# A product with V cut in two, ended by the products of 1/sum, and a new order table

## The chip, the cores and the metric

The kernel runs on one core of one Trainium2 chip. The metric is the device time of one execution in microseconds (us). Before the change it was 1055.64 us, the median of three runs (1054.31 to 1058.27).

The core has five engines that run side by side and meet only at semaphores. In profiles they are PE (TensorE, matrix products; its weight loads are shown as PEld), DVE (VectorE), ACT (ScalarE), POOL (GpSimd) and SP (SyncE, which issues transfers). Each runs its own instructions in a fixed order.

## The reference

An attention with rotary embedding over 8 batches of 8 heads (576 positions, 64 per head), and behind it a channel mix with squared ReLU and a sigmoid gate:

```python
scores = scale * np.matmul(q_rot, k_rot.transpose(0, 1, 3, 2))
scores = scores - np.max(scores, axis=-1, keepdims=True)
attn = np.exp(scores)
attn = attn / (np.sum(attn, axis=-1, keepdims=True) + 1e-09)
x = np.matmul(attn, v)          # then the heads side by side: (8, 576, 512)
...
xk = mu_k * x + (1.0 - mu_k) * x_prev      # x_prev: one position earlier
xr = mu_r * x + (1.0 - mu_r) * x_prev
k = np.maximum(xk @ w_k, 0.0)
v = k * k @ w_v
r = 1.0 / (1.0 + np.exp(-(xr @ w_r)))
return r * v
```

All arrays are float32.

## The kernel before

Attention works on 32 pairs of heads, four pairs to a batch; the channel mix works on 16 half batches of 288 positions. Below, V1 to V32 are the products with V of the 32 pairs.

For each pair, `plan_rope` loads k and q and rotates them (L328 to L332; the operations go through the helper `combine`, L241). `plan_unit` is one of five units of scores: matmuls on TensorE into PSUM tiles `s` (L373), their row maximum on VectorE (L382, tile `nm`), the exponential and its sum on ScalarE (L385, tile `p`), and a transpose of 32x32 blocks on VectorE (L388). `plan_ratio` makes 1/sum and spreads it into the tile `rw` (L413 to L417). `plan_values` multiplies with V: 144 calls of `matmul` on 32-row tiles (L447), which the trace shows as 288 matmuls and 288 weight loads, and then eight calls that spread 1/sum over PSUM in the same way (L454). `plan_total` copies the spread 1/sum to SBUF (ScalarE, L467, tile `rp`), multiplies it with the product (VectorE, L472 to L474, tile `xT`), and hands on the border column (POOL, L479 to L483).

In the channel mix, `plan_mix` forms mu*x + (1-mu)*x_prev and splits it into a high and a low part (L517 to L522, L245, L247, L241), and `plan_product` multiplies with the weights, three matmuls for each step of the sum: high by high, low by high, high by low (L547 to L549, tile `acc`). The weights come as 64-bit words; `plan_convert` turns each of 20 blocks into a high and a low float32 part with eight instructions on VectorE, ScalarE and POOL (L278 to L295 and the helpers).

The order on each engine comes out of a planner. Each operation has a rank: a due time of its pair or half batch (18 rank units a pair), and an offset for its kind from the table `R`. `Plan.issue` plays the program through with a planned duration for each operation and, whenever an engine is free, gives it the ready operation of the lowest rank. Where an operation may run on several engines, it goes to the one that takes it first, with the `B_` numbers as a handicap. Operations marked as shared use the SBUF read interface that VectorE and POOL have in common: in the plan one of them starts only when the other's has ended. Buffers are granted in the order of rank: three PSUM tiles `s`, of which a product with V takes two, and a single tile for V (`vs`).

The lines that set the order and the two parts of the product:

```python
_, i = heapq.heappop(queue)
...
o = op("T", t, 2 * NB * 137 + 330, values, need, slots + [d["sp"], d["sv"]])
o = op("T", t + 0.01, 2 * 137, shares, [o, d["R"]], slots + [d["srw"]])
```

Of the kernel before, what the change touches and what calls it, by code (L numbers as in the profile page):

```python
# [13 lines left out]
F32 = mybir.dt.float32  # L14
# [10 lines left out]
R = dict(k=28.88, q=62.36, v=55.38, cs=-59.77, ld=36.87, rope0=-101.48, rope1=58.83, rope2=-126.74, split0=-113.91,  # L25
         split1=433.88, u0=-9.3, u1=-10.62, u2=4.58, u3=-7.12, u4=4.34, mx=2.38, ex=86.96, rs=95.84, dg=-55.12,
         bd=122, tr=-72.26, ev=352.37, av=9.08, tot=24.45, bor=5.22, m0=68.43, mh=-2.22, mk=13.02, mr=26.57, ms=1.29,
         tp=149.1, rz=62.63, rc=93.12, mx1=-27.44, mx2=-52.23, mx3=35.89, mg=3.02, mv=-2.35, dr=-78.45, key0=8.16,
         key1=19.5, key2=110.59, gate0=-83.54, gate1=264.13, wk0=-8.35, wk1=-9.74, wr0=-255.69, wr1=-10.63, wv0=-20.6,
         wv1=9.46)  # L30
PB = (-68.11, -8.23, -7.76, -4.01, -5.06, -7.72, 1.05, -20.98)
B_COPY, B_ROPE, B_SPLIT, B_LOW, B_MIX, B_SQUARE, B_RELU, B_SMALL = -365.18, 42.18, -112.3, 217.28, 11.6, -103.75, 494.08, 91.52
MB = (14.69, 13.58, 6.65, 1.17, 2.36, 19.06, 26.3, 392.46)
CY = 12
BUFS = dict(nat=2, kh=2, kl=2, qh=2, ql=2, vs=1, pt=2, s=3, nm=6, sums=2, rs=2, rw=1, rp=2, xT0=4, xT1=4, last=5, raw=1, we=1, wm=1, mxf=2, mxh=5, mxl=5, acc=2, hr=2, kkh=8, kkl=8, rt=3)
# [18 lines left out]
def pool(n):  # L54
    return 2.15 * n + 160

# [7 lines left out]
class Plan:  # L64
# [15 lines left out]
    def op(self, engine, rank, cost, fn, after=(), uses=()):  # L80
# [10 lines left out]
        self.ops.append((engine, rank, None, fn, tuple(after), tuple(uses), opens))  # L91
# [7 lines left out]
    def issue(self):  # L99
# [23 lines left out]
        now, engine = 0.0, {}  # L123

# [67 lines left out]
def rope_attention_channel_mix(ctx, tc, qt, kt, v, cs, mu, w_k, w_v, w_r, out):  # L192
# [28 lines left out]
    def f32(ap):  # L221
        return ap.bitcast(F32)
# [77 lines left out]
    def plan_weights(w, hi, lo, t0, t1):  # L300
# [5 lines left out]
            (c, n): plan_convert(t0 + i * (t1 - t0) / len(blocks), words[c * P:(c + 1) * P, 2 * n:2 * n + 1024], hi[:, c, n:n + 512], lo[:, c, n:n + 512])  # L306
# [6 lines left out]
    def plan_rope(t, d, n, src, plain):  # L313
# [395 lines left out]
```

## Time and profile before

| | |
|---|---|
| median of three runs | 1055.64 us |
| the profiled execution, whole | 1059.64 us |
| its span, first to last instruction | 1057.8 us |
| mean granted clock of TensorE | 0.955 |
| instructions | 34,697 |
| TensorE idle in the span | 100.7 us (1057.8 - 957.1) |
| of that up to 165 us | 67.2 us (165.0 - 97.77) |
| read from HBM, written | 88.74 MB, 9.44 MB |

The page gives, for each engine, its busy time and its number of instructions, and the span in 40 slices of 26.4 us, where a digit is the busy share in tenths. A group row reads: line, engine, operation, what it writes and what it reads, shapes, count; then busy us and the mean of one in ns; then the idle time of the engine just before and what ended it. "issue" stands where the engine waited for nothing that the profile shows.

### The profile page before, as it was taken

What the parts mean: (1) busy time and instruction counts of PE and PEld (TensorE: products, weight loads), DVE (VectorE), ACT (ScalarE), POOL (GpSimd) and SP (SyncE); (2) the same over time, 40 slices, a digit from 0 to 9 for tenths busy, and PEclk for the clock granted to TensorE, in tenths of its full rate; (3) what the DMA queues carried; (4) which work ended last, traced back from release to release, by engine and by line L of the source; (5) the groups of instructions that cost most, each with busy time, mean ns of one, the idle gap of its engine ahead of it and who ended that gap; (6) DMA issues with size and microseconds to landing.
All of it is one profiled execution on the core that took longest, in us unless ns stands there. A gap on an engine that the chain in (4) does not pass through costs nothing.

```text
span 1057.8 us, 34697 instructions
## 1 busy us (share of the span) xinstructions
PE 957.1 (90%) x15134; PEld 841.9 (80%) x15134; DVE 845.9 (80%) x1483; ACT 537.0 (51%) x1330; POOL 479.9 (45%) x556
## 2 busy tenths in 40 slices
PE   2676478999899999999999999999999999999998
PEld 1454256878788888888888888888888888988998
DVE  7898889869498888788788887778887988776552
ACT  2343436637175565537475555546474655645243
POOL 5544336445264463536374464437453535322111
PEclk9957667999999999999999999999999999999999
DMA  6333332241312233132322233132322233211000
GB/s 246 112 127 130 133 128 85 72 158 41 140 55 105 106 99 111 53 133 73 108 94 79 94 106 105 53 133 78 134 72 72 94 106 105 82 59 54 18 23 24
DMA packets 30456, 100.41 MB, mean 95 GB/s; under 512 B 3040, under 2 KB 11232, under 8 KB 26208
## 3 DMA queue, kind: packets, MB, share of 16 engines
q1 hardware_dynamic: 30304, 98.19, 26.6%
q8 instruction: 119, 1.95, 0.8%
q14 instruction: 33, 0.27, 0.1%
HBM read 88.74 MB, written 9.44 MB: 93 GB/s over the span
## 4 chain that ended last, share of the span: by engine, by line
PE 79%; DVE 13%; issue 4%; ACT 2%; DMA 1%; POOL 1%; DVEq 0%; POOLq 0%; ACTq 0%
PE av L447 18%; PE acc L547 17%; PE acc L548 14%; PE acc L549 14%; PE s L373 13%; DVE nm L382 3%; DVE p L388 2%; PE av L454 2%; ACT p L385 1%; DVE wm L294 1%; DMA raw<-in_w_r 1%; DVE wm L295 1%; DVE mxf L522 1%; DVE wm L282 1%; DVE we L278 1%
## 5 line engine op out<-in xcount | busy, mean ns | idle before, releaser
L385 ACT ACTIVATE p<-s,nm 128x576 f32<-128x576 f32 x288 | 211.4, 737 | 133.6 <-DVE nm L382 132.0
L447 PE MATMUL av<-p,values 32*64 32x160 f32 (+1 forms) x9216 | 192.3, 305 | 38.3 <-issue 22.6
L447 PEld LDWEIGHTS av<-p,values 32*64 32x64 f32 x9216 | 171.9, 136 | 56.5 <-issue 36.2
L382 DVE TENSOR_REDUCE nm<-s 128x1 f32<-128x576 f32 x288 | 205.3, 744 | 14.0 <-PE s L373 13.0
L388 DVE STREAM_TRANSPOSE p<-p 128x576 f32<-128x576 f32 x288 | 210.1, 752 | 5.0 <-ACT p L385 4.8
L373 PE MATMUL s<-kh,qh 64*128 64x288 f32 (+1 forms) x738 | 147.5, 438 | 49.2 <-POOL qh L241 29.0
L547 PE MATMUL acc<-mxh,wk_h 128*128 128x288 f32 x512 | 160.5, 313 | 3.0 <-DVE rt L603 1.4
L547 PE MATMUL acc<-kkh,wv_h 128*128 128x288 f32 x512 | 159.2, 311 | 1.5 <-DVE rt L603 0.9
L373 PEld LDWEIGHTS s<-kh,qh 64*128 64x128 f32 (+1 forms) x738 | 81.9, 212 | 97.6 <-ACT p L385 32.0
L549 PE MATMUL acc<-mxh,wk_l 128*128 128x288 f32 x512 | 151.5, 296 | 1.3 <-POOL wk_l L241 1.3
L548 PE MATMUL acc<-mxl,wk_h 128*128 128x288 f32 x512 | 152.1, 297 | 0.2 <-POOL mxl L241 0.2
L548 PE MATMUL acc<-kkl,wv_h 128*128 128x288 f32 x512 | 151.5, 296 | 0.0
L549 PE MATMUL acc<-kkh,wv_l 128*128 128x288 f32 x512 | 151.2, 295 | 0.0
L241 POOL TENSOR_TENSOR mxl<-mxf,mxh 128x288 fp32r<-128x288 f32 x89 | 79.1, 900 | 100.7 <-DVE mxh L247 71.2
L547 PEld LDWEIGHTS acc<-mxh,wk_h 128*128 128x128 f32 x512 | 96.9, 189 | 20.4 <-issue 14.0
L547 PEld LDWEIGHTS acc<-kkh,wv_h 128*128 128x128 f32 x512 | 96.4, 188 | 16.8 <-issue 11.1
L241 POOL TENSOR_TENSOR kkl<-hr,kkh 128x288 fp32r<-128x288 f32 x95 | 85.7, 910 | 35.6 <-ACT kkh L245 22.2
L467 ACT COPY rp<-av 128x320 f32<-128x320 f32 x64 | 25.1, 428 | 144.6 <-PE av L454 144.1
L549 PEld LDWEIGHTS acc<-mxh,wk_l 128*128 128x128 f32 x512 | 97.0, 189 | 1.7 <-POOL wk_l L241 1.7
L548 PEld LDWEIGHTS acc<-mxl,wk_h 128*128 128x128 f32 x512 | 97.2, 190 | 0.6 <-POOL mxl L241 0.4
L548 PEld LDWEIGHTS acc<-kkl,wv_h 128*128 128x128 f32 x512 | 96.8, 189 | 0.1
L549 PEld LDWEIGHTS acc<-kkh,wv_l 128*128 128x128 f32 x512 | 96.7, 189 | 0.0
(91 smaller groups left out, 1772.1 us busy)
## 6 DMA issues: line engine op xcount, KB each, us to landing
values<-in_v SPq DMA_DIRECT2D x32, 1152.0 KB, 5.1
xq<-in_qt SPq DMA_DIRECT2D x32, 640.0 KB, 4.5
xk<-in_kt SPq DMA_DIRECT2D x32, 576.0 KB, 4.2
out_dram<-rt SPq DMA_DIRECT2D x64, 144.0 KB, 1.8
raw<-in_w_v SPq DMA_DIRECT2D x8, 512.0 KB, 3.2
raw<-in_w_k SPq DMA_DIRECT2D x8, 512.0 KB, 3.3
raw<-in_w_r SPq DMA_DIRECT2D x4, 512.0 KB, 3.3
turn<-in_cs SPq DMA_DIRECT2D x1, 640.0 KB, 4.4
```

The source lines that it names most:

```text
L241: (V if e == "V" else G).tensor_tensor(out=out, in0=a, in1=b, op=op)
L278: V.tensor_scalar(out=u("e"), in0=d["high"], scalar1=20, scalar2=0x7FF, op0=ALU.logical_shift_right, op1=ALU.bitwise_and)
L373: T.matmul(w[x][:, h, 0:H], lhsT=kind(d[q][r, c * P:(c + 1) * P]), rhs=kind(d[k][r, h * H:(h + 1) * H]), start=i == 0, stop=i == len(todo) ...
L382: V.tensor_reduce(out=w["nm", x], in_=w[x][:, :, 0:H], op=ALU.max, axis=AX.XY, negate=True)
L385: A.activation(halves(d["pt"][:, place]), w[x][:, :, 0:H], AF.Exp, bias=w["nm", x], scale=1.0, accum_out=d["sums"][:, place + 1:place + 2])
L388: V.transpose(d["pt"][:, place], d["pt"][:, place])
L447: T.matmul(at(a, x, c0, 32 * (p1 - p0)), lhsT=d["vf"][g, b * P + x * D:b * P + x * D + D], rhs=d["pt"][g, p0:p1, 32 * b:32 * b + 32], star ...
L454: T.matmul(at(a, x, 256, 160), lhsT=first_row[g], rhs=d["rw"][g, p0 + 1:p1 + 1], start=True, stop=True)
L467: A.copy(w["r", half], w[half][:, :, 256:416])
L547: T.matmul(w["a"], lhsT=w_h[:, i, sl], rhs=x["h"], start=(i == 0), stop=False)
L548: T.matmul(w["a"], lhsT=w_h[:, i, sl], rhs=x["l"], start=False, stop=False)
L549: T.matmul(w["a"], lhsT=w_l[:, i, sl], rhs=x["h"], start=False, stop=(i == count - 1))
```

## The change

Four things are changed.

1. The 144 calls of the product with V are two operations of the planner: blocks 0 to 8 (72 calls) and blocks 9 to 17 with the eight products of 1/sum behind them. The second has a rank of its own (`av2`) and waits for 1/sum. Before, the first operation held all 144 calls, and only the eight products waited for 1/sum.
2. When `Plan.issue` picks for VectorE or POOL, each shared operation is ranked later by 0.1353 units for each ns that the other engine will still hold the interface.
3. The first six pairs have offsets of their own for 19 kinds of operation (`EARLY`), and each of the 20 weight blocks has one (`WORDS`); the numbers of `R`, `PB`, `MB` and the handicaps are new.
4. The planned duration of a product on TensorE follows a model of the array (half rate while cold, a cost for a new tile shape, a least time for each 256 instructions), and some planned durations on ScalarE and VectorE differ. That alters only the order.

What is computed is the same, instruction for instruction on TensorE; on VectorE, ScalarE and POOL operations move between engines.

```diff
-R = dict(k=28.88, q=62.36, v=55.38, cs=-59.77, ld=36.87, rope0=-101.48, rope1=58.83, rope2=-126.74, split0=-113.91,
+R = dict(k=44.27, q=66.09, v=57.3, cs=-364.48, ld=64.17, rope0=112.51, rope1=437.99, rope2=-790.69, split0=-68.32,
...
+NE = 6
+EARLY = dict(k=(-430.77, -247.46, -0.16, -62.14, -67.11, -4.22), q=(-124.45, -334.75, -23.13, -18.46, 21.08, 35.02),
...
+WORDS = dict(wk=(-119.65, 277.59, -356.19, -160.94, -146.41, 45.43, 67.45, -152.52), wr=(-120.79, -322.22, -307.35,
...
+CUT = 9
+WAIT = 0.1353
...
+def lead(name, pair):
+    return R[name] + (EARLY[name][pair] if pair < NE else 0)
...
-                    _, i = heapq.heappop(queue)
+                    if e in port:
+                        held = max(0.0, port["G" if e == "V" else "V"] - now)
+                        best = min(queue, key=lambda r: (r[0] + (WAIT * held if r[1] not in engine and ops[r[1]][0][e][2] else 0), r[1]))
+                        queue.remove(best)
+                        heapq.heapify(queue)
+                        _, i = best
+                    else:
+                        _, i = heapq.heappop(queue)
...
+                    if e == "T":
+                        cost = product_time(start, cost, ops[i][2])
...
-        def values():
-            for half in range(2):
-                w[half] = ps.tile([P, 2, 512], F32, tag="s", name="av", bufs=BUFS["s"])
-            for b in range(NB):
+        def values(b0, b1):
+            if b0 == 0:
+                for half in range(2):
+                    w[half] = ps.tile([P, 2, 512], F32, tag="s", name="av", bufs=BUFS["s"])
+            for b in range(b0, b1):
...
-        o = op("T", t, 2 * NB * 137 + 330, values, need, slots + [d["sp"], d["sv"]])
-        o = op("T", t + 0.01, 2 * 137, shares, [o, d["R"]], slots + [d["srw"]])
+        def rest():
+            values(CUT, NB)
+            shares()
+
+        o = op("T", t, 2 * CUT * 144, lambda: values(0, CUT), need, slots + [d["sp"], d["sv"]], ("row", 32 * CUT))
+        o = op("T", t + lead("av2", d["pi"]), 2 * (NB - CUT) * 144 + 2 * 137, rest, [o, d["R"]], slots + [d["sp"], d["sv"], d["srw"]], ("row", 32 * (NB - CUT) + 32))
```

`product_time` is the new model: it takes the planned cost of one TensorE operation and returns the planned time.

```python
def product_time(start, cost, shape):
    kind, count = shape
    ...
    if not array["warm"]:
        cost *= 1.9
    end = start + 220 * (kind != array["shape"])
    array["shape"] = kind
    while count:
        step = min(count, 256 - array["place"])
        end += cost * step / shape[1]
        count -= step
        array["place"] += step
        if array["place"] == 256:
            array["place"] = 0
            end = max(end, array["line"])
            array["line"] = end + 3000
    ...
    return end - start
```

Three places show how the orders differ. The changed file has other line numbers: L432 there is L373, L441 is L382, L447 is L388, L479 is L420, L476 is L417, L507 is L447, L514 is L454, L536 to L538 are L472 to L474, L611 to L613 are L547 to L549, L299 and L305 are the helpers L241 and L247, and L336, L340, L344, L352 and L353 are L278, L282, L286, L294 and L295.

First, TensorE at the end of V16, in the middle of the span. Before, three weight matmuls stand between the 144 calls with V and the eight calls with `first_row`, which spread 1/sum:

```order
L447 MATMUL av<-p,values 64x128
L447 MATMUL av<-p,values 64x160
L547 MATMUL acc<-kkh,wv_h 128x288
L548 MATMUL acc<-kkl,wv_h 128x288
L549 MATMUL acc<-kkh,wv_l 128x288
L454 MATMUL av<-rw,first_row 64x160 x8
L547 MATMUL acc<-mxh,wk_h 128x288
```

In the changed program the three stand in the middle of V16, between its two halves; the eight calls with `first_row` follow the second half directly:

```order
L507 MATMUL av<-p,values 64x128
L507 MATMUL av<-p,values 64x160
L611 MATMUL acc<-kkh,wv_h 128x288
L612 MATMUL acc<-kkl,wv_h 128x288
L613 MATMUL acc<-kkh,wv_l 128x288
L507 MATMUL av<-p,values 64x160
L507 MATMUL av<-p,values 64x128
```

The group of three has moved from behind the product into it; it is so from V5 to V32, while the halves of V1 to V4 touch.

Second, TensorE between V3 and V4. Before, 26 score matmuls follow V3, 18 of pair 4 and then eight of pair 5, and V4 comes behind them:

```order
L454 MATMUL av<-rw,first_row 64x160 x8
L373 MATMUL s<-kh,qh 128x288 x26
L447 MATMUL av<-p,values 64x160
L447 MATMUL av<-p,values 64x128
L447 MATMUL av<-p,values 64x160
```

In the changed program the score matmuls of pair 4 end directly ahead of V4, and six weight matmuls stand among them:

```order
L514 MATMUL av<-rw,first_row 64x160 x8
L432 MATMUL s<-kh,qh 128x288 x8
L611 MATMUL acc<-mxh,wk_h 128x288
L612 MATMUL acc<-mxl,wk_h 128x288
L613 MATMUL acc<-mxh,wk_l 128x288
L432 MATMUL s<-kh,qh 128x288 x6
L611 MATMUL acc<-mxh,wk_h 128x288
L612 MATMUL acc<-mxl,wk_h 128x288
L613 MATMUL acc<-mxh,wk_l 128x288
L432 MATMUL s<-kh,qh 128x288 x4
```

The score matmuls of pair 5 have moved behind V4, and the first weight matmuls ahead of it (before, the first of all stand behind V4).

Third, VectorE ahead of the totals of pair 4 (the first `xT` row of each piece, which needs V4). Before, the last transposes of pair 4 stand 29 instructions earlier, and the maxima and transposes shown here are those of pair 5:

```order
L388 STREAM_TRANSPOSE p<-p 128x576
L241 TENSOR_TENSOR xk<-xk,turn 128x576
L382 TENSOR_REDUCE nm<-s 128x1 x2
L388 STREAM_TRANSPOSE p<-p 128x576 x3
L278 TENSOR_SCALAR we<-raw 128x512
L282 TENSOR_SCALAR wm<-raw 128x512
L294 SCALAR_TENSOR_TENSOR wm<-raw,wm 128x512
L295 SCALAR_TENSOR_TENSOR wm<-raw,wm 128x512
L286 TENSOR_TENSOR wm<-wm,we 128x512
L247 CAST wk_h<-wm 128x512
L241 TENSOR_TENSOR wk_l<-wm,wk_h 128x512
L472 TENSOR_TENSOR xT_1361<-av,rp 128x2x128
```

In the changed program the transpose in the first row is the last of pair 4, and nine instructions stand between it and the totals:

```order
L447 STREAM_TRANSPOSE p<-p 128x576
L305 CAST wk_h<-wm 128x512
L299 TENSOR_TENSOR wk_l<-wm,wk_h 128x512
L299 TENSOR_TENSOR xk<-xk,turn 128x576 x2
L336 TENSOR_SCALAR we<-raw 128x512
L340 TENSOR_SCALAR wm<-raw 128x512
L352 SCALAR_TENSOR_TENSOR wm<-raw,wm 128x512
L353 SCALAR_TENSOR_TENSOR wm<-raw,wm 128x512
L344 TENSOR_TENSOR wm<-wm,we 128x512
L536 TENSOR_TENSOR xT_1358<-av,rp 128x2x128
```

The maxima and transposes of pair 5 have moved behind the totals of pair 4; the conversion of weights fills the place.

More of the change, by code (lines that the diff above doesn't have):

```diff
@@ L78, in slot, with op @@
         return slots[-1]
-    def op(self, engine, rank, cost, fn, after=(), uses=()):
+    def op(self, engine, rank, cost, fn, after=(), uses=(), shape=("full", 0)):
         o = len(self.ops)
@@ L90, in op @@
             s.opener = o
-        self.ops.append((engine, rank, None, fn, tuple(after), tuple(uses), opens))
+        self.ops.append((engine, rank, shape, fn, tuple(after), tuple(uses), opens))
         return o
@@ L123, in issue @@
         now, engine = 0.0, {}
+        array = dict(shape="full", place=0, line=0.0, warm=False, window=0, busy={})
+        def product_time(start, cost, shape):
+            kind, count = shape
+            window = int(start // 3413)
+            for w in range(array["window"], window):
+                share = array["busy"].get(w, 0.0) / 3413
+                array["warm"] = share > 0.95 or share > 0.6 and array["warm"]
+            array["window"] = window
+            if not array["warm"]:
[11 more added lines that the diff above has]
+                    array["line"] = end + 3000
+            at = start
+            while at < end:
+                w = int(at // 3413)
+                to = min(end, (w + 1) * 3413)
+                array["busy"][w] = array["busy"].get(w, 0.0) + to - at
+                at = to
+            return end - start
         def met(i):
@@ L335, in plan_rope @@
         sl = Slot(n + "l")
[L336 removed]
+        r = op(two(w, B_ROPE), t + lead("rope2", pi), 0, lambda e: combine(e, m["c"], m["c"], m["s"], ALU.add), [ms, mc], [slot])
         h = op(one(w, B_SPLIT), t + R["split0"], 0, lambda e: copy(e, part(n + "h"), m["c"]), [r], [slot, sh])
@@ L373, in products @@
                         T.matmul(w[x][:, h, 0:H], lhsT=kind(d[q][r, c * P:(c + 1) * P]), rhs=kind(d[k][r, h * H:(h + 1) * H]), start=i == 0, stop=i == len(todo) - 1)
-        m = op("T", t, (8 if d["plain"] else 6) * (120 + 14) + (360 if c < 4 else 0), products, d["q"] + d["k"], slots + d["sq"] + d["sk"])
+        m = op("T", t, (8 if d["plain"] else 6) * (120 + 12), products, d["q"] + d["k"], slots + d["sq"] + d["sk"], ("row" if c < 4 else "full", (8 if d["plain"] else 12) * len(heads)))
         for x in heads:
@@ L483, in border @@
                 G.tensor_copy(xT[:, 0:1], d["last"])
-        o = op("A", t + R["rc"] + 0.1 * half, act(320) + 60, copied, [o], [slot, s_r])
-        o = op("V", t + R["tot"] + 0.1 * half, dve(256) + 2 * 105, total, [o], [slot, s_r, sx])
+        o = op("A", t + lead("rc", d["pi"]) + 0.1 * half, act(320) + 60, copied, [o], [slot, s_r])
+        o = op("V", t + lead("tot", d["pi"]) + 0.1 * half, dve(256) + 2 * 210 + 30, total, [o], [slot, s_r, sx])
         if half == 0:
@@ L553, in plan_product @@
             x, h, l, s_h, s_l = hold[parts, i]
-            prev = [op("T", t + i * dt, pe(n, 3), lambda i=i, x=x: group(i, x), [h, l, done[i, m * P // 512 * 512]] + prev, [s_a, s_h, s_l])]
+            prev = [op("T", t + i * dt, pe(n, 3), lambda i=i, x=x: group(i, x), [h, l, done[i, m * P // 512 * 512]] + prev, [s_a, s_h, s_l], ("full", 6))]
         return w, s_a, prev[0], t + count * dt
@@ L633, in rope_attention_channel_mix @@
     plan_attention()
-    wk_done = plan_weights(w_k, wk_h, wk_l, R["wk0"], R["wk1"])
-    wr_done = plan_weights(w_r, wr_h, wr_l, R["wr0"], R["wr1"])
-    wv_done = plan_weights(w_v, wv_h, wv_l, R["wv0"], R["wv1"])
+    wk_done = plan_weights(w_k, wk_h, wk_l, R["wk0"], R["wk1"], "wk")
+    wr_done = plan_weights(w_r, wr_h, wr_l, R["wr0"], R["wr1"], "wr")
+    wv_done = plan_weights(w_v, wv_h, wv_l, R["wv0"], R["wv1"], "wv")
     for b in range(B):
```

67 lines of the change are left out of this document (39 added, 28 removed).

## The prediction

> **What bounds the kernel now.** I first read the page's busy shares and slices, to see which engine is full and when.
>
> ```profile
> PE 957.1 (90%) x15134; PEld 841.9 (80%) x15134; DVE 845.9 (80%) x1483; ACT 537.0 (51%) x1330; POOL 479.9 (45%) x556
> PE   2676478999899999999999999999999999999998
> PEclk9957667999999999999999999999999999999999
> q8 instruction: 119, 1.95, 0.8%
> ```
>
> TensorE is full from the eighth slice on; in the first seven (185 us) it idles, partly at a low granted clock. The average of 90% therefore joins two stages. The table by stretches, cut where the products change, separates them (its columns are stretch, length, then busy us and count for PE, PEld, DVE, ACT and POOL, and the clock).
>
> ```profile
> 0.00:165.00 165.00, 97.77 (x1397) 65.23 (x1397) 142.13 (x216) 63.23 (x136) 78.26 (x82) 0.75 0.40 143
> 165.00:215.00 50.00, 45.88 (x573) 40.04 (x579) 45.99 (x78) 31.67 (x75) 26.82 (x28) 0.95 0.24 80
> 215.00:261.00 46.00, 43.64 (x550) 36.59 (x540) 36.73 (x59) 24.95 (x66) 21.06 (x25) 0.96 0.28 99
> 261.00:347.00 86.00, 82.19 (x1372) 72.46 (x1370) 66.10 (x123) 41.52 (x105) 41.97 (x48) 0.98 0.29 100
> 347.00:977.00 630.00, 610.27 (x10617) 551.17 (x10616) 516.55 (x925) 347.93 (x884) 299.01 (x360) 1.00 0.27 92
> ```
>
> Up to 165 us TensorE loses 67 us and VectorE is 86% busy: the start belongs to VectorE. From 347 us TensorE is 97% busy, so only its own work and its own stalls count there. Third view: what TensorE waited for, over the whole span (total, times, longest).
>
> ```profile
> PE s L373 <- POOL qh L241: 29.0, 3, 15.9
> PE av L447 <- issue: 22.6, 30, 2.2
> PE s L373 <- ACT p L385: 16.4, 12, 2.8
> PE av L447 <- DVE p L388: 12.1, 2, 6.7
> PE av L454 <- issue: 3.6, 6, 1.3
> PE acc L547 <- DVE rt L603: 2.3, 7, 0.7
> ```
>
> The waits for other engines are almost all of the start. The 26.2 us called "issue" are different: inside the product with V, TensorE stops although all its data is there, some 30 times. The timeline of one product (start, duration, instructions merged) shows how.
>
> ```profile
> 278.63 2.94 PE L447 MATMUL av<-p,values 32*64 32x160 f32 x153
> 282.07 2.42 PE L447 MATMUL av<-p,values 32*64 32x128 f32 x128 [0.50 <-issue]
> 285.52 0.50 PE L447 MATMUL av<-p,values 32*64 32x128 f32 x7 [1.03 <-issue]
> 285.95 0.40 PE L547 MATMUL acc<-kkh,wv_h 128*128 128x288 f32 x1
> ```
>
> The two stops are exactly 128 matmuls apart. Each matmul has a weight load, so that is 256 instructions, and 30,268 matmuls and loads over the 119 instruction transfers of queue q8 are 254 per transfer. I read this as TensorE outrunning its instruction supply: 128 of these matmuls take 2.42 us, while the next block came 3.45 us after the one before (285.52 - 282.07).
>
> [...]
>
> **The change, part by part.**
>
> *Split of the product with V.* A block filled with these matmuls alone lacks 3.45 - 2.42 = 1.0 us, less what TensorE's queue had in hand (0.50 us lost at the first stop, 1.03 at the second). Counting 256-instruction blocks along both orders, with the phase of the stops above, after the first five products: before has 35 blocks of V matmuls alone and 11 with one group of three weight matmuls; the change has 20 and 28. So the 22.6 us on L447 are some 0.6 us for each block of the first kind, and L454's 3.6 us some 0.3 for each of the second. If those prices held, the saving would be 15 x 0.6 - 17 x 0.3 = 4 us. But before's second kind mostly came after a stop, with nothing in hand; in the change it comes first in the burst, and the group of weight matmuls (0.6 us: 0.5 from 542.62 to a step past 542.99 in the rows below, 0.1 for the change into it) fills most of the gap. At no loss there and 0.6 for the rest the saving is 26 - 12 = 14 us. I take 9, the middle; the ends are 4 and 14.
>
> *The wait for 1/sum ahead of the second half.* Queued behind it on TensorE are the half itself and all that follows. No row shows L447 or L454 waiting for rw, and 1/sum stands at most seven VectorE instructions behind the last transpose in both orders. Its cover is the first half and the weight group, some 3 us. I price it at nothing; if VectorE were that late, each 1 us would cost up to 1 us in each of 32 products.
>
> *More changes between products.* TensorE changes tile shape 388 times instead of 359; 14 of the 29 lie behind the tenth product with V, where nothing hides them.
>
> ```profile
> 541.27 0.29 PE L548 MATMUL acc<-mxl,wk_h 128*128 128x288 f32 x1
> 541.40 0.29 PE L549 MATMUL acc<-mxh,wk_l 128*128 128x288 f32 x1
> 541.63 0.53 PE L373 MATMUL s<-kh,qh 64*128 64x288 f32 x4
> 542.62 0.40 PE L547 MATMUL acc<-mxh,wk_h 128*128 128x288 f32 x1
> 542.86 0.30 PE L548 MATMUL acc<-mxl,wk_h 128*128 128x288 f32 x1
> 542.99 0.29 PE L549 MATMUL acc<-mxh,wk_l 128*128 128x288 f32 x1
> ```
>
> Weight matmuls step 0.13 us; at a change the step is 0.23 and 0.24, so 0.1 more. 14 to 29 changes cost 1.4 to 2.9 us: **+2**.
>
> *The start.* The sixth product with V (V6) is where TensorE last stands directly behind VectorE:
>
> ```profile
> 213.78 0.78 DVE L388 STREAM_TRANSPOSE p<-p 128x576 f32<-128x576 f32 x1 [0.27 <-ACT p L385]
> 214.80 3.33 PE L447 MATMUL av<-p,values 32*64 32x160 f32 x177
> ```
>
> Ahead of that transpose VectorE has 291 instructions before and 284 in the change. Priced by their groups' means they come to 201.6 and 200.1 us (overlap counted twice): **-1.5**. What those instructions lose to POOL is larger:
>
> ```profile
> L282 DVE TENSOR_SCALAR wm<-raw x20: 403/416/1767, 4.4 to 196.0; 128x512 uint32<-128x512 uint32 x20
> L388 DVE STREAM_TRANSPOSE p<-p x288: 710/762/781, 22.3 to 971.7; 128x576 f32<-128x576 f32 x144
> L294 DVE SCALAR_TENSOR_TENSOR wm<-raw,wm x20: 641/682/1916, 4.8 to 196.8; 128x512 uint32<-128x512 uint32 x20
> ...
> L294 DVE SCALAR_TENSOR_TENSOR wm<-raw,wm 128x512 uint32<-128x512 uint32 x20 | 17.0, 848 | 0.2
> L282 DVE TENSOR_SCALAR wm<-raw 128x512 uint32<-128x512 uint32 x20 | 14.1, 707 | 0.0
> L278 DVE TENSOR_SCALAR we<-raw 128x512 uint32<-128x512 uint32 x20 | 13.6, 679 | 3.7 <-DMA raw<-in_w_r 3.6
> ```
>
> The first three rows give the shortest, median and longest of a line, the others count, busy us and mean. L388 is never stretched; L282 runs from 403 to 1767 ns. Against a median of 416 its 20 lose 5.8 us, L278's likewise 5.3, and L294's 3.3: 14.4 us on 60 instructions, 0.24 each. Some 140 of the 291 are of the kinds that the planner marks as sharing the interface (136 in the change), so about 33 us are lost by V6. [...]
>
> The new rule of the planner passes over such instructions while the other engine holds the interface. It acts on planned times, and it can only pick others that are ready. I take a third of the loss, **-11**; the ends are -25 (three quarters of it) and +8 (planned gaps that do not fall where planned). The wait of VectorE for POOL or ScalarE at the totals I leave as it is: in pair 1 the order puts ten instructions ahead of L472 instead of five, but in pair 4 only nine instead of 29.
>
> Against this, the change has done fewer weight matmuls by V6, 192 instead of 219, and as many (735) by V10. These 27 come later at 0.133 us each: **+3.6**. Before, ten score matmuls stand ahead of V4 and wait for POOL, with V4's own operands done:
>
> ```profile
> 125.87 2.08 DVE L388 STREAM_TRANSPOSE p<-p 128x576 f32<-128x576 f32 x3
> 135.32 3.24 PE L373 MATMUL s<-kh,qh 64*128 64x288 f32 x10 [12.31 <-POOL qh L241]
> 141.54 0.79 PE L447 MATMUL av<-p,values 32*64 32x160 f32 x4
> ```
>
> In the change those of pair 5 stand behind V4. That brings weight work forward into the idle start, but V6 waits for VectorE all the same, so I give it nothing. The first product, V1, now waits for more transposes (30 score matmuls ahead of it, not 18); this too lies ahead of V6.
>
> *Moved work and transfers.* VectorE gives 43 instructions away, mostly to ScalarE and POOL (25 more on POOL). Behind 347 us TensorE's 610 of 630 us cover it, worth nothing; were that cover gone, POOL's 25 at the 0.91 us of its most frequent form would cost 23. SP issues the same loads in another order, the early ones above all, and the values tile is held a weight group longer ahead of its next load of 5.1 us; the products with V are 33 us apart (1057.8 / 32), so I price this at nothing too.
>
> ```profile
> L241 POOL TENSOR_TENSOR kkl<-hr,kkh 128x288 fp32r<-128x288 f32 x95 | 85.7, 910 | 35.6 <-ACT kkh L245 22.2
> values<-in_v SPq DMA_DIRECT2D x32, 1152.0 KB, 5.1
> ```
>
>
> **The sum.** -9 + 2 - 1.5 - 11 + 3.6 = -16. The profiled execution took 1059.64 us (span 1057.8), 4.0 above the median of 1055.64: it becomes 1043.6, and on the median's scale **1040**.
>
> **The rivals.**
>
> *The start stays.* Planned gaps miss, VectorE loses 33 us as before: -9 + 2 - 1.5 + 3.6 = -5, so 1051. For it: the trace does not run as planned. In the first 215 us VectorE sat idle for 12.5 us ahead of totals that its order put too early:
>
> ```profile
> DVE xT L472 <- ACT rp L467: 12.5, 4, 4.6
> ```
>
> 16%.
>
> *Most of the interface wait goes.* -25 in place of -11: 1026. For it: half of VectorE's work in the start does not share, so there is often something to pick. 15%.
>
> *The stops only move.* If what a burst no longer waits for is waited for in its second half or behind it, the split is worth 0: -7, so 1049. The 128 matmuls between the rows at 282.07 and 285.52 speak against it. [...] 5%.
>
> *Slower: V6 comes later.* Between V5 and V6 the change leaves TensorE 51 weight matmuls, not 105, some 7 us of work at full clock. So each us by which VectorE is late there is an idle us of TensorE, with a low clock behind it. If the interface loss grows instead of shrinking, it decides from +5 on, where the saved stops are used up; at half as much again (+17) the sum is +12, 1068. For it: POOL is given more to do. Against it: 136 sharing instructions, not more. 8%.
>
> **How the numbers follow.** My forecast holds 56%, with 1032 to 1048 as its own range. What a measurement of this kernel can tell from no change is about 0.5%, 5.3 us: faster is below 1050.4. The forecast, the second and third rival and half of the first make 84%; the other half of the first is 8% within; the last 8%. The range, 1022 to 1054, reaches through the first rival and nearly to the second's centre and leaves out about 6% below and 10% above.
>
> **What would show it.** The split: "PE av L447 <- issue" falls from 22.6 to some 13 us. The start: V6 begins near 202 us, and L282's mean falls from 707 toward 600 ns. Later: no row of the second half waiting for rw, and TensorE at 97% from V10 on. I am wrong if stops stay near 22 us, if V6 lies behind 215, or if TensorE shows waits for other engines after V10.

## The result, and the profile after

| | before | after |
|---|---|---|
| median of four runs each | 1056.95 us | **1027.61 us** (1026.29 to 1029.71) |
| ratio, with its 95% interval | | 0.9721 [0.9683, 0.9759] |
| the profiled execution, whole | 1059.64 us | 1027.46 us |
| its span | 1057.8 us | 1025.6 us |
| mean granted clock | 0.955 | 0.970 |
| V6 begins, V10 begins | 214.8, 347.0 us | 199.1, 327.6 us |

The change gains 2.8%, about 29 us by the medians and 32.2 us between the two profiled executions. Of those 32.2 us, 15.7 are there when V6 begins, 3.7 more when V10 begins (347.0 - 327.6 = 19.4 together), and 12.9 come behind V10 (from V10 to the end 710.8 us before, 697.9 after). Times and ratios, here and below, leave out one execution of `more_vector_late` that took 4874 us; all others lie within 1.5% of the fastest of their kernel.

The page of the changed kernel: busy time of each engine, TensorE's slices and granted clock, and the instruction queue.

```profile
PE 940.8 (92%) x15134; PEld 836.7 (82%) x15134; DVE 834.6 (81%) x1440; ACT 544.6 (53%) x1348; POOL 498.1 (49%) x581
PE   2667687999999999999999999999999999999998
PEclk9987668999999999999999999999999999999999
q8 instruction: 119, 1.95, 0.8%
```

TensorE's program has the same 15,134 matmuls, and 16.3 us less busy time (957.1 - 940.8). The low digits end about as early as before, but fewer of them stand below 9. The table by stretches, cut where V6 and V10 begin, first of the kernel before, then of the changed one (stretch, length, busy us and count of PE, PEld, DVE, ACT and POOL, granted clock, DMA share, GB/s).

```profile
0.00:214.80 214.80, 143.45 (x1956) 105.07 (x1956) 187.92 (x293) 94.89 (x211) 105.08 (x109) 0.79 0.36 128
214.80:347.00 132.20, 126.03 (x1921) 109.26 (x1920) 103.03 (x181) 66.47 (x170) 63.03 (x72) 0.97 0.29 100
```

```profile
0.00:199.12 199.12, 135.41 (x1928) 101.22 (x1928) 180.44 (x291) 86.18 (x199) 97.85 (x108) 0.85 0.41 142
199.12:327.60 128.48, 125.38 (x1946) 110.26 (x1945) 107.10 (x183) 71.25 (x181) 66.71 (x77) 1.00 0.28 98
...
347.00:945.00 598.00, 584.21 (x10212) 532.41 (x10213) 495.97 (x862) 350.35 (x880) 309.90 (x366) 1.00 0.27 94
```

Up to V6, VectorE has nearly the same number of instructions (293 and 291), is busy for 7.5 us less with them and idle for 8.2 us less (26.9 and 18.7 us). TensorE is idle 7.6 us less and runs at a higher clock. From V6 to V10 its clock is 1.00 instead of 0.97, which is worth less than 2 us (`start_old` below takes 130.4 us there, in the order of before and at a clock of 1.00). Behind V10 TensorE is 97.7% busy.

What TensorE waited for, in the changed kernel, from the start to 347 us and from there on (total, times, longest); first the early part.

```profile
PE av L507 <- DVE p L447: 18.3, 5, 5.0
PE s L432 <- POOL qh L299: 17.2, 1, 17.2
PE s L432 <- ACT p L444: 10.4, 9, 1.9
PE acc L611 <- DVE wk_h L305: 6.3, 1, 6.3
```

```profile
PE av L514 <- issue: 10.3, 9, 1.6
PE av L507 <- issue: 2.2, 8, 0.6
PE acc L612 <- issue: 1.0, 1, 1.0
PE acc L611 <- DVE rt L667: 0.2, 1, 0.2
```

Two of the three waits for the rotated q (qh) are gone: 29.0 us in three waits became 17.2 in one. Late in the span the other engines make TensorE wait for 0.4 us in all; what is left are the stops called "issue", and they now stand mostly in the products of 1/sum (L514), no longer in the product with V (L507). Over the whole span they were 3.6 us in the products of 1/sum and 22.6 in the product with V; now they are

```profile
PE av L514 <- issue: 13.5, 13, 1.6
PE av L507 <- issue: 4.6, 10, 1.4
```

No row names rw, and in the trace rw is done 3.1 us or more before any second half begins, so the wait for 1/sum costs nothing. The timeline of V17 shows the new place of a stop (start, duration, instructions merged).

```profile
521.74 2.73 PE L507 MATMUL av<-p,values 32*64 32x160 f32 x144
524.39 0.40 PE L611 MATMUL acc<-mxh,wr_h 128*128 128x288 f32 x1
...
524.99 2.82 PE L507 MATMUL av<-p,values 32*64 32x160 f32 x142
...
527.74 0.34 PE L514 MATMUL av<-rw,first_row 32*64 32x160 f32 x5
529.37 0.49 PE L514 MATMUL av<-rw,first_row 32*64 32x160 f32 x4 [1.29 <-issue]
529.78 0.40 PE L611 MATMUL acc<-mxh,wr_h 128*128 128x288 f32 x1
```

Each half runs through without a stop. Then TensorE stops: the last four products of 1/sum begin 1.63 us after the five before them, and 1.40 us after an instruction transfer that lands at 527.97. The profile calls 1.29 us of that idle. Not every product has this stop: V6 takes 6.4 us in all, V17 8.0 (529.78 - 521.74), and the products behind V10 take either 6.3 to 6.9 us or 7.7 to 8.4.

That these stops are waits for instructions can be seen in the trace, which has the start and the duration of each of the 119 instruction transfers of queue q8. Every one of the 23 idle stops called "issue" on L507 and L514, and every one of the 36 of the kernel before, ends 1.2 to 1.6 us after such a transfer has landed; a random instant of the kernel before lies 0 to 33 us behind the last landing, 4.5 in the median. The 3.45 us between two blocks in the prediction's timeline also come apart: from 282.07 it is 1.1 us until the next transfer starts, the transfer takes 0.9, and 1.4 us after its landing TensorE goes on at 285.52.

The last place where TensorE stands behind VectorE has also moved. Two rows of VectorE's timeline, and two of TensorE's:

```profile
162.34 1.64 DVE L305 CAST wk_h<-wm 128x512 fp32r<-128x512 f32 x1
...
189.52 0.43 DVE L305 CAST wv_h<-wm 128x512 fp32r<-128x512 f32 x1
...
194.89 0.78 DVE L447 STREAM_TRANSPOSE p<-p 128x576 f32<-128x576 f32 x1 [0.40 <-ACT p L444]
```

```profile
164.13 0.58 PE L611 MATMUL acc<-mxh,wk_h 128*128 128x288 f32 x1 [6.31 <-DVE wk_h L305]
...
199.12 2.73 PE L507 MATMUL av<-p,values 32*64 32x160 f32 x144
```

V6's last transpose ends at 195.67, 3.4 us ahead of V6; before, 0.2 us ahead. The last wait for another engine of over 1 us is now the one that ends at 164.13, for a converted block of weights. The cast that ends it took 1.64 us, beside an instruction of POOL that ran from 161.66 to 163.70; the same cast of another block took 0.43 at 189.52. So 1.2 of the 6.3 us are this stretch.

### The profile page after: what moved, and what is told of

Same layout as the page of the kernel before. It is cut to its first block, busy times and chain, and to the rows that moved or that the text cites. A ratio compares the mean times of both kernels' runs of the same rounds, so it can differ in the third digit from the quotient of the medians.

```text
span 1025.6 us, 34670 instructions
## 1 busy us (share of the span) xinstructions
PE 940.8 (92%) x15134; PEld 836.7 (82%) x15134; DVE 834.6 (81%) x1440; ACT 544.6 (53%) x1348; POOL 498.1 (49%) x581
## 4 chain that ended last, share of the span: by engine, by line
PE 84%; DVE 11%; issue 3%; DMA 1%; ACT 1%; POOL 0%; SPq 0%; DVEq 0%; POOLq 0%; ACTq 0%
PE acc L611 20%; PE av L507 16%; PE acc L612 16%; PE acc L613 16%; PE s L432 14%; DVE p L447 2%; DVE nm L441 2%; PE av L514 1%; DVE wm L352 1%; DVE wm L353 1%; DMA turn<-in_cs 1%; DVE we L336 1%; DVE wm L340 1%; DVE wm L344 0%; DVE mxf L586 0%
## 5 line engine op out<-in xcount | busy, mean ns | idle before, releaser
L441 DVE TENSOR_REDUCE nm<-s 128x1 f32<-128x576 f32 x288 | 205.2, 745 | 27.1 <-PE s L432 25.3
L447 DVE STREAM_TRANSPOSE p<-p 128x576 f32<-128x576 f32 x288 | 210.3, 754 | 7.9 <-ACT p L444 7.8
L507 PE MATMUL av<-p,values 32*64 32x128 f32 (+1 forms) x9216 | 194.2, 303 | 23.1 <-DVE p L447 18.3
L507 PEld LDWEIGHTS av<-p,values 32*64 32x64 f32 x9216 | 168.6, 136 | 42.2 <-DVE p L447 21.6
L432 PE MATMUL s<-kh,qh 64*128 64x288 f32 (+1 forms) x738 | 140.6, 427 | 34.1 <-POOL qh L299 17.2
L611 PE MATMUL acc<-mxh,wk_h 128*128 128x288 f32 x512 | 163.4, 319 | 6.5 <-DVE wk_h L305 6.3
L611 PE MATMUL acc<-kkh,wv_h 128*128 128x288 f32 x512 | 157.6, 308 | 1.9 <-issue 1.0
L613 PE MATMUL acc<-mxh,wk_l 128*128 128x288 f32 x512 | 152.6, 298 | 0.0
L613 PE MATMUL acc<-kkh,wv_l 128*128 128x288 f32 x512 | 150.7, 294 | 0.0
L299 POOL TENSOR_TENSOR mxl<-mxf,mxh 128x288 fp32r<-128x288 f32 x98 | 87.1, 896 | 117.9 <-ACT mxh L303 98.1
L432 PEld LDWEIGHTS s<-kh,qh 64*128 64x128 f32 (+1 forms) x738 | 79.6, 207 | 75.3 <-ACT p L444 19.6
L299 POOL TENSOR_TENSOR kkl<-hr,kkh 128x288 fp32r<-128x288 f32 x107 | 95.2, 897 | 76.2 <-ACT kkh L303 59.2
L611 PEld LDWEIGHTS acc<-mxh,wk_h 128*128 128x128 f32 x512 | 98.0, 191 | 25.4 <-issue 20.4
L611 PEld LDWEIGHTS acc<-kkh,wv_h 128*128 128x128 f32 x512 | 96.0, 188 | 13.4 <-issue 10.0
L586 DVE SCALAR_TENSOR_TENSOR mxf<-xT,mu_t,mxf 128x288 f32<-128x288 f32 x128 | 89.3, 715 | 18.5 <-ACT mxf L581 17.3
L613 PEld LDWEIGHTS acc<-mxh,wk_l 128*128 128x128 f32 x512 | 98.1, 192 | 0.2 <-DVE wk_l L299 0.2
L613 PEld LDWEIGHTS acc<-kkh,wv_l 128*128 128x128 f32 x512 | 96.2, 188 | 0.0
```

Source lines behind the costliest of these rows:

```text
L299: (V if e == "V" else G).tensor_tensor(out=out, in0=a, in1=b, op=op)
L432: T.matmul(w[x][:, h, 0:H], lhsT=kind(d[q][r, c * P:(c + 1) * P]), rhs=kind(d[k][r, h * H:(h + 1) * H]), start=i == 0, stop=i == len(todo) ...
L441: V.tensor_reduce(out=w["nm", x], in_=w[x][:, :, 0:H], op=ALU.max, axis=AX.XY, negate=True)
L447: V.transpose(d["pt"][:, place], d["pt"][:, place])
L507: T.matmul(at(a, x, c0, 32 * (p1 - p0)), lhsT=d["vf"][g, b * P + x * D:b * P + x * D + D], rhs=d["pt"][g, p0:p1, 32 * b:32 * b + 32], star ...
L586: V.scalar_tensor_tensor(out=x["f"], in0=d["x", half][:, 1:1 + n], scalar=mu_t[:, m:m + 1], in1=x["f"], op0=ALU.mult, op1=ALU.add)
```

## The experiments

In nine of the twelve kernels, `split_only` to `more_vector_late`, the planner's order is fixed: they are the changed file with a list of the operations in the order in which they were issued, so that one piece can be moved while all else stays. Their line numbers differ: L539 is L373 of the kernel before, L548 is L382, L551 is L385, L554 is L388, L614 is L447, L621 is L454 and L720 to L722 are L547 to L549. In the schematic diffs V(a,b) stands for the blocks a to b-1 of a product with V, W for three weight matmuls, S for the eight products of 1/sum. The last three kernels are the files themselves with one edit. The ratio is against runs of the kernel before on the same chip: one chip for the first four rows, another for the next four, a third for the last four. The last three columns are the starts of V6 and V10 and the end of the span in one profiled execution.

| kernel | median us | ratio, 95% interval | V6 | V10 | end |
|---|---|---|---|---|---|
| split_only | 1045.68 | 0.9857 [0.9821, 0.9894] | 213.8 | 345.3 | 1045.8 |
| unsplit | 1044.62 | 0.9858 [0.9824, 0.9891] | 199.7 | 330.5 | 1042.9 |
| start_new | 1043.07 | 0.9839 [0.9797, 0.9882] | 199.2 | 327.7 | 1043.4 |
| start_old | 1044.86 | 0.9870 [0.9819, 0.9921] | 214.4 | 344.8 | 1042.4 |
| same_chip_before | 1057.11 | 0.9988 [0.9961, 1.0015] | 211.9 | 342.2 | 1057.3 |
| same_chip_after | 1028.02 | 0.9714 [0.9689, 0.9740] | 199.4 | 328.4 | 1029.2 |
| second_break | 1029.27 | 0.9724 [0.9705, 0.9743] | 196.9 | 326.6 | 1026.1 |
| more_vector_early | 1035.99 | 0.9790 [0.9768, 0.9812] | 207.7 | 336.3 | 1036.6 |
| more_vector_late | 1035.45 | 0.9780 [0.9734, 0.9825] | 198.9 | 328.5 | 1033.7 |
| no_port_rule | 1056.53 | 0.9974 [0.9951, 0.9998] | 212.5 | 343.2 | 1054.6 |
| no_early_ranks | 1038.55 | 0.9806 [0.9761, 0.9852] | 208.2 | 340.6 | 1039.4 |
| port_rule_alone | 1066.37 | 1.0075 [1.0045, 1.0106] | 214.5 | 346.8 | 1065.1 |

### The split alone, and all but the split

`split_only` is the order of before with only the product cut:

```diff
-V(0,18)
+V(0,9)
 W
+V(9,18)
 S
```

> The order of before, instruction for instruction, with one thing changed: the second nine blocks of each product with V stand behind the weight matmuls that stood ahead of the products of 1/sum. Theory A (the supply of instructions sets the pace inside the product, and a group of weight matmuls in its middle gives it time): TensorE's issue stops fall from 26 to 16-20 us, the start stays, time 1047 to 1051. Rival B (the stops only move to the second half and the products of 1/sum): stops stay near 26 us, time 1055 to 1059.

`unsplit` is the changed kernel's order with the product whole again:

```diff
-V(0,9)
+V(0,18)
 W
-V(9,18)
 S
```

> The order of the changed kernel with the split alone undone: all 144 calls with V in one piece, the weight matmuls behind them as before. Theory A: the 22 bursts from V10 to V31 go back from 7.19 to about 7.5 us each, 7 us and a little for V5 to V9, time 1034 to 1038. Rival B: stops only moved, time 1026 to 1030.

The split alone brings 1060.47 - 1045.68 = 14.8 us against before on its chip, and nothing up to V10 (345.3 us, against 344.8 in `start_old`, which has the order of before up to there). All but the split brings 1.42%, 15 us. Both times lie outside what was expected (1047 to 1051 and 1034 to 1038 us), since the split is worth more than was thought. The two add: 0.9857 x 0.9858 = 0.9717, within the interval of the whole. The waits of TensorE, first of `split_only`, then of `unsplit`, show where the stops stand.

```profile
PE av L621 <- issue: 12.5, 12, 1.3
PE av L614 <- issue: 7.8, 8, 1.7
```

```profile
PE av L614 <- issue: 22.5, 30, 1.2
PE av L621 <- issue: 5.5, 12, 0.8
```

The split takes the stops from 26.2 us in 36 places (before) to 20.3 in 20. That is 5.9 us for a gain of 14.8, so the idle time doesn't hold the whole price. It is counted from the modelled end of the instruction before, and a matmul of the product lasts 0.29 us in the median: in all 28 of these stops behind V10 in the kernel before, the step from start to start is the idle time and 0.29 us more. I therefore added up the steps from start to start among the matmuls of L447 and L454 behind V10: all those over 0.12 us, less the 0.019 us of an ordinary step. Before, that is 31.2 us. The idle rows of the same stretch of the kernel before are

```profile
PE av L447 <- issue: 14.2, 23, 1.1
PE av L454 <- issue: 2.4, 5, 0.6
```

which is 16.6 us, little more than half. On the chip of these four kernels, and behind V10 too, `start_new` (there the order of before, product whole) has 35.0 us by steps and 21.1 by idle time, and `split_only` 19.4 and 10.8. By steps the split saves 15.6 us, which is its gain; by idle time it would be 10.3.

### Which half of the time the rest belongs to

`start_new` issues the changed kernel's order up to V10, then all that is left in the order of before, with the product whole. `start_old` is the reverse, with the split from V10 on.

```diff
-issue(new)
+issue(until(new, "V10") + left(old))      # start_new
+issue(until(old, "V10") + left(new))      # start_old
```

> The changed order up to the start of V10, the old order (product whole) from there. Theory A (the gains add: 19 us by V10, 13 behind it): V10 starts near 328 us, from there as in before, time 1036 to 1040. Rival C (the start only shifts work that the old rest then waits for): V10 near 328 but more than 715 us from V10 to the end, time above 1045.

> The old order up to the start of V10, the changed order with its split from there. Theory A (gains add): V10 near 347 us, 698 us from there to the end instead of 711, time 1042 to 1046. Rival C (the later gain comes from the better start): V10 near 347 and 705 us or more behind it, time 1050 or more.

`start_new` reaches V10 at 327.7 us like the changed kernel, and `start_old` at 344.8. The gains, 1.61% and 1.30%, make 2.9% together: the start's gain isn't eaten later, and what comes behind V10 doesn't need the new start. `start_new` is slower than the 1036 to 1040 us expected, and its 715.7 us behind V10 are just above the 715 that were named for rival C; but `same_chip_before`, with the old start, takes 715.1 there, so the new start is not the reason. The four kernels of this chip also part the stretch from V10 to the end by its two edits:

| V10 to the end, us | product whole | product cut | difference |
|---|---|---|---|
| order of before | 715.7 (`start_new`) | 700.5 (`split_only`) | 15.2 |
| order of the change | 712.5 (`unsplit`) | 697.6 (`start_old`) | 14.9 |
| difference | 3.2 | 2.9 | |

The split is worth 15 us there in either order, and the new order 3. In steps from start to start, the products with V and of 1/sum with the changes of shape into them fall from 162.9 to 149.5 us in the upper row and from 162.0 to 148.8 in the lower: 13 of the 15 us lie inside the products themselves.

### The two orders on one chip

Nothing is edited in these two: the fixed lists are the orders of before and of the change.

```diff
 issue(old)      # same_chip_before
 issue(new)      # same_chip_after
```

> The kernel before, in its own order, once more: a profile of it on the same chip as the next three. Issue stops and the length from V10 to the end show how far two chips differ; 711 us from V10 to the end if they do not, 715 if the supply of instructions is slower on some chips, as the 7.7 us bursts of the last runs suggest.

> The changed kernel in its own order on the same chip. If the parts add (split 15, the rest 16 us by the last four runs): 31 us below the kernel before. If they overlap: 25 or less.

By the medians the change gains 29.1 us on this chip (1057.11 - 1028.02), and 31.0 against the runs of the file itself (1059.01), so the parts add. On one chip V6 gains 12.5 us, V10 13.8, and the stretch behind V10 14.3 (715.1 to 700.8). In the pair of profiles above they were 15.7, 19.4 and 12.9, and on the chip of the table 18 behind V10 (715.7 - 697.6): from pair to pair, single stages differ by 3 to 6 us. Part of it may be the clock. In the profile of `same_chip_before` the granted clock is 0.95 from 169 us to the end, where the others have 1.00 behind V10. The median step of its weight matmuls is 132 ns all the same, but the 144 matmuls of a half product start within 2.49 us instead of 2.42, some 3 us over the 46 halves behind V10 (an estimate, 46 x 0.07).

### A second break in the product

If a group of weight matmuls inside a product is worth its place because it lengthens the block, a second one should help where a product spans three block borders. In 13 products the next group was moved in as well, in the others the first was moved to the middle of its block.

```diff
 V(0,c1)
 W
-V(c1,18)
+V(c1,c2)
+W
+V(c2,18)
 S
```

> The changed order; in those 13 products with V that reach over three block borders the next group of weight matmuls also stands inside, and the first break is put in the middle of the first whole block. Theory A: 13 blocks of V matmuls alone become mixed ones, at 0.6 to 1.0 us of stop each, and each further break costs 0.3 us of tile shape changes: 4 to 9 us faster than the changed kernel. Rival B (stops only move): slower than it by 13 x 0.3 = 4 us.

No gain: 0.9724 against 0.9714 on the same chip. The profile shows why. Behind V10 the steps of L614 and L621 do fall, by 6.5 us (143.8 to 137.3, start to start). The steps into a product and back to weight matmuls rise by 4.5 us (10.0 to 12.3 and 31.4 to 33.6), since each group inside brings two more changes of tile shape, and the remaining steps by 0.7. The cure costs most of what it saves: 1.3 us are left behind V10 (700.8 to 699.5), and none in the median.

### VectorE's time ahead of V6, and far behind it

Five transposes are done three times, ahead of V6 in one kernel and ahead of V21 in the other: ten more transposes, some 7 us of VectorE.

```diff
 turned(unit)
+turned(unit)
+turned(unit)
```

> The changed order; five of the nine transposes ahead of V6 are each done three times (the result is the same), 7 us more work for VectorE. Theory A (V6 is set by VectorE, and what comes later there is never made up): V6 and the end 7 us later than the changed kernel. Rival D (TensorE has other work and makes it up): V6 up to 7 us later, the end less than 3 us later.

> The changed order; five of the nine transposes ahead of V21 are each done three times, 7 us more work for VectorE in the middle of the span. Theory A (behind V10 TensorE sets the pace and VectorE has room): the end less than 2 us later than the changed kernel, 1028 to 1031 on the chip of its first measurement. Rival E (VectorE is near its limit there too): 5 to 7 us later.

Ahead of V6 the 7 us move V6 by 8.3 us, and the end by 7.4. So VectorE still sets the start in the changed kernel, and what is lost there is never made up. It is not V6's last transpose that holds V6 (it ends 3.5 us ahead in `same_chip_after` and 4.9 here); up to V6, TensorE's waits for the exponentials grow from 10.8 to 14.4 us, and one of 0.8 us for a converted block of weights is new.

Ahead of V21 I had thought them hidden, and they aren't: 0.9780 against 0.9714. The two ratios are from two chips and their intervals touch, so the traces have to decide. V21 begins 6.3 us later than in `same_chip_after`, V20 only 1.6 later, and the delay stays. Two rows of VectorE's timeline, the same two in `same_chip_after`, and then two of TensorE's in `more_vector_late`:

```profile
609.37 4.66 DVE L554 STREAM_TRANSPOSE p<-p 128x576 f32<-128x576 f32 x6
613.95 1.38 DVE L548 TENSOR_REDUCE nm<-s 128x1 f32<-128x576 f32 x2
```

```profile
607.73 1.41 DVE L554 STREAM_TRANSPOSE p<-p 128x576 f32<-128x576 f32 x2
609.07 1.37 DVE L548 TENSOR_REDUCE nm<-s 128x1 f32<-128x576 f32 x2
```

```profile
612.62 0.48 PE L614 MATMUL av<-p,values 32*64 32x160 f32 x4
615.59 4.29 PE L614 MATMUL av<-p,values 32*64 32x160 f32 x140 [2.49 <-ACT p L551]
```

Six transposes stand in a row instead of two, and the row maximum behind them comes 4.9 us later (613.95 against 609.07), of which 1.6 is V20's own delay. V20 takes two of the three PSUM tiles, and by the releaser that the profile names the second was still being read by the exponential of that maximum. So 3.3 us more on VectorE's path became a wait of 2.5: it had 0.8 us in hand. And the delay is 4.7 us (6.3 - 1.6), not 2.5. The table by stretches of 1 us has the rest (columns as above):

```profile
614.00:615.00 1.00, 0.00 (x0) 0.00 (x0) 1.00 (x3) 0.30 (x1) 0.00 (x0) 1.00 0.00 0
615.00:616.00 1.00, 0.41 (x16) 0.42 (x24) 1.00 (x3) 1.00 (x3) 0.00 (x0) 0.73 0.00 0
616.00:617.00 1.00, 1.00 (x49) 1.00 (x38) 1.00 (x3) 0.26 (x2) 0.80 (x1) 0.50 0.00 0
617.00:618.00 1.00, 1.00 (x40) 1.00 (x32) 0.97 (x3) 0.00 (x0) 1.00 (x1) 0.50 0.02 8
```

The granted clock falls to 0.50 and is back at 1.00 by 619; with 0.73 in the stretch from 615 and 0.56 in that from 618 it is at 0.50 for 3.4 us. The half product that runs in this time takes 4.29 us instead of 2.73, so 1.6 more. Start to start, from the half to the weight matmuls behind it, it is 7.19 us instead of 2.66, which is 4.5 of the 4.7. So here a clock of 0.50 followed a wait of 2.5 us. The length of a stop does not decide alone whether the clock falls: in the kernel before, the 1.62 us that ended at 268.03 were followed by 3.4 us at 0.50, from 269.27 on, while 2.21 and 2.11 us in `port_rule_alone` (ended at 220.05 and 267.74) left it at 1.00.

### The planner's rule and the early ranks

`no_port_rule` is the changed kernel without the planner's rule for the shared interface; `no_early_ranks` is without the offsets of the first six pairs; `port_rule_alone` is the kernel before with the rule only.

```diff
-WAIT = 0.1353
+WAIT = 0.0
```

> The changed kernel planned with WAIT = 0, so that a held interface no longer ranks an operation later; the tables stay. If the rule makes the start better: by V6 VectorE loses 30 us or more to POOL, not 27, V6 lies at 205 us or later, time 1033 to 1045. If it does nothing by itself: V6 near 199 and time within 3 us of the changed kernel. The tables were made with the rule, so a loss can also be that of a plan that no longer fits.

```diff
-NE = 6
+NE = 0
```

> The changed kernel planned without own offsets for the first six pairs (NE = 0); those of the weight blocks, the rule and the split stay. If the early offsets carry the start: V6 at 210 us or later, time above 1040; the part behind V10 stays near 698 us. If not: V6 near 199.

```diff
+WAIT = 0.1353
...
-                    _, i = heapq.heappop(queue)
+                    if e in port:
+                        held = max(0.0, port["G" if e == "V" else "V"] - now)
+                        best = min(queue, key=lambda r: (r[0] + (WAIT * held if r[1] not in engine and ops[r[1]][0][e][2] else 0), r[1]))
+                        queue.remove(best)
...
```

> The kernel before with the rule alone (WAIT = 0.1353), old tables, product whole. If the rule by itself keeps VectorE from waiting for POOL: the loss by V6 falls from 35 us to below 30 and V6 comes 5 us or more earlier than 214 us, time 1045 to 1052. If it only works with tables made for it: no gain or a loss, 1055 to 1075.

Without the rule the new tables are worth almost nothing, although the split is in: V6 comes at 212.5, and 1056.5 us are far above the 1033 to 1045 expected. Late in the span TensorE now waits for other engines again, here in the answer from 347 us on:

```profile
PE acc L612 <- POOL mxl L299: 1.6, 3, 0.7
PE s L432 <- ACT p L444: 1.2, 4, 0.4
PE s L432 <- DVE xT L538: 1.1, 1, 1.1
PE acc L611 <- DVE rt L667: 1.1, 4, 0.5
PE acc L611 <- ACT rp L531: 1.0, 1, 1.0
```

These and two smaller ones are 6.9 us, where the changed kernel has 0.4, and from V10 to the end `no_port_rule` takes 13.5 us longer (711.4 against 697.9). With the rule on the old tables nothing falls at V6 (214.5), and 1.0075 is a small loss.

The rule does act on what it is meant for, but only together with the tables. I took, for every instruction of VectorE ahead of V6 of the kinds that the planner marks as sharing the interface, its duration less the eighth percentile of its form in the trace of before. That loss is 35.0 us before, 26.9 after, 34.6 in `no_port_rule`, 35.7 in `port_rule_alone` and 32.0 in `no_early_ranks`. So rule and tables were fitted to each other, and neither is worth anything alone at V6; what each "contributes" can't be told from these runs. Only the early offsets can be named: without them V6 is 9 us later (208.2, a little less than expected) and the time behind V10 the same (698.8). The new planned durations and the offsets of the weight blocks were never taken out alone, so their share stays open.

## Why the prediction was right, and where its sizes were off

**Sign, range and mechanisms.** The forecast was 1040 with 1022 to 1054; the result is 1027.6. Both mechanisms that carried it are there and act where it said: the stops of TensorE's instruction supply, and VectorE's loss to POOL ahead of V6. The sum was -16 and the profiles show -32 (the medians -29), so nearly half of the gain was missed. That the range held is in part luck: 1027.6 lies outside the forecast's own 1032 to 1048, next to the second rival's 1026, but that rival's mechanism, a loss to POOL that shrinks by 25 us, isn't what happened. Two other steps were too small, the split and the wait at the totals. Step by step:

**The split, -9 (4 to 14).** The mechanism is right, the size is not: 15 us, just past the upper end. The step that failed is the price. It took the idle time of the "issue" rows, 0.6 us for a block, and start to start the stops cost nearly twice that (31.2 against 16.6 us behind V10). L507's stops fell to 4.6 us, not to some 13, since most of what is left stands on L514. The rival by which the stops only move was therefore half true: those on L514 rose from 3.6 us to 13.5. But all together fell from 26.2 us to 18.1, and by that rival `split_only` would have equalled before, where it gained 1.4%.

**The wait for 1/sum, 0.** Right; no row names rw.

**Shape changes, +2.** Right in sign, but smaller: behind V10 the changed steps are 2.6 us more in all, on 14 of them, of which the ordinary steps they replace are more than half; that leaves about 1 us.

**VectorE's count, -1.5.** Right: up to V6's last transpose it is 291 instructions before and 284 after. VectorE is busy for 10.4 us less up to there (186.9 to 176.5), of which some 8 are the loss to POOL of the next step and 2 are left. That transpose ends 18.9 us earlier (214.56 to 195.67), V6 only begins 15.7 earlier, since it now stands 3.4 us behind it.

**The loss to POOL, -11 (-25 to +8).** -8.1 between the two profiles, -6.8 between the two orders on one chip (32.2 to 25.4). That POOL is the cause can be seen in the kernel before: ahead of V6, of VectorE's TENSOR_SCALAR, TENSOR_TENSOR and SCALAR_TENSOR_TENSOR instructions all 34 that lose over 0.2 us run beside an instruction of POOL, and the 82 that run beside none lose at most 0.05. So these two engines meet not only at semaphores. The traces show the stretch, not what causes it inside; a common read interface is what the planner assumes. The groups on which it was based now read, on VectorE (count, busy us, mean ns, idle before):

```profile
L352 DVE SCALAR_TENSOR_TENSOR wm<-raw,wm 128x512 uint32<-128x512 uint32 x20 | 15.0, 750 | 0.3
L340 DVE TENSOR_SCALAR wm<-raw 128x512 uint32<-128x512 uint32 x20 | 11.6, 581 | 0.0
```

848 ns became 750, and 707 became 581, near the 600 that was named as the sign.

**The wait at the totals, "as it is".** This is the step that failed at the start. The 12.5 us that VectorE lost ahead of the totals fell to

```profile
DVE xT L536 <- ACT rp L531: 1.5, 2, 0.9
```

I weighed one pair with more instructions ahead against one with fewer, and called it even. What counts is whether the product with V has run by the time the totals stand at the head. Before, VectorE was free for the totals of pairs 1 to 4 between 1.5 and 4.2 us before the product with V and its spread 1/sum were done; in the new order it is between 0.4 us before and 2.3 behind. VectorE's idle time ahead of V6 fell by 8.2 us in all, as much as its loss to POOL.

**The 27 weight products that come later, +3.6.** They come later, and yet V6 to V10 got 3.7 us shorter (132.2 to 128.5). In steps from start to start the weight matmuls take 1.8 us more there and the four products V6 to V9 5.0 us less (29.7 to 24.7), as TensorE's idle time is 3.1 us instead of 6.2. These four belong to the split's term, so here too it was too small, but only some 2 us are the split: on one chip V6 to V10 is 128.6 us in the new order with the product cut (`start_new`) and 130.8 with it whole (`unsplit`). The rest came with the new order, by which way is open: with the product whole the four take 26.5 us in it and 30.0 in the old one (`start_old`). The granted clock, 1.00 instead of 0.97, is not the main cause: the old order at 1.00 takes 130.4 and 131.5 us (`start_old`, `split_only`) and at 0.95 130.3 (`same_chip_before`), where before took 132.2.

**Moved work, 0.** Right for the change as it is: behind V10 TensorE waits 0.4 us for other engines. But the cover that I named, TensorE's share of 97%, is no cover. `more_vector_late` shows that 7 us more on VectorE cost some 5 to 7 us, and `no_port_rule` that the same work in a worse order costs TensorE 6.9 us of waits there. I was right because the order is good, not because TensorE is full.

**What stays open.** The ordinary steps between weight matmuls behind V10 take 4 to 5 us less in the new order, with the split and without (on one chip 414.2 and 412.6 us in the order of before, 409.0 and 408.1 in that of the change; 0.9 of it is that there are seven fewer). Between the two profiles some 3 of the 5 us are long steps, 17 of together 5.5 us before and five of 2.4 after. The rows of the kernel before name VectorE's `rt` in six waits of together 2.1 us behind V10; what the other long steps waited for stays open.

## What to carry to other kernels

Price a stop of TensorE from start to start, in the timeline, and not by its idle time: where many short matmuls overlap, the profile's idle column showed little more than half of what the stops cost (16.6 of 31.2 us). TensorE at 97% didn't make VectorE's work free: 7 us more of it cost some 5 to 7. Ask how late a single result may come before a tile is held, since that slack was 0.8 us in the one place that was measured, and the wait of 2.5 us that followed cost 4.7. A rule in a planner and the table fitted with it are one part: test them together and apart before saying which of them helped.

## What the runs showed of the hardware that was not expected

- A wait of TensorE of 2.5 us was followed by 3.4 us at a granted clock of 0.50, a delay of 4.7 us in all (`more_vector_late`). A stop of 1.62 us in the kernel before was followed by the same 3.4 us, and stops of 2.11 and 2.21 us in `port_rule_alone` were not.
- Each stop called "issue" in the products, 36 before and 23 after, ended 1.2 to 1.6 us after an instruction transfer had landed. Of the 3.45 us from block to block that one product showed, the transfer itself took 0.9.
- With the same work, the changed kernel's products with V behind V10 take 6.3 to 6.9 us, or 7.7 to 8.4 where a stop of 1.0 to 1.6 us stands in the products of 1/sum. In V17, 144 matmuls of one half run through in 2.73 us.
- Breaking 13 of the bursts a second time saved 6.5 us of stops and cost 4.5 in shape changes, and the median did not fall.
- One stretched instruction stood where TensorE waited: the cast (L305) that ended the 6.3 us wait took 1.64 us instead of 0.43, so 1.2 of them are its stretch.
